# Delta-rule attention and an MLP mixer on one core: two products of a fast matrix scheme change places, one chain gets a bank of its own, and the second half of the order is written anew

## The chip, the cores and the metric

The kernel runs on one core of a Trainium2 chip. A core has engines that work at the same time, each from a queue of its own in the order in which the program issued: TensorE (PE; its weight loads, PEld, overlap its matmuls), VectorE (DVE), ScalarE (ACT), GpSimd (POOL) and SyncE (SP), which issues the transfers (DMA) between HBM and the on-chip memory. TensorE writes to PSUM banks; the others read them. An instruction starts when those before it on its engine have started and what it waits for on other engines is done.

The metric is the device time of one execution in microseconds, lower is better. Data are fp32. A matmul of 128x128 by 128x192 leaves two records of PE in the profile (two passes), so a product of two such matmuls has four.

## The reference

```python
def _attn_ref(q, k, v, beta):                      # B 4, H 8, S 768, D 48
    k_n = k / (np.linalg.norm(k, axis=-1, keepdims=True) + 1e-06)
    state = np.zeros((B, H, D, D), dtype=np.float32)
    for t in range(S):
        kt, vt, bt = (k_n[:, :, t], v[:, :, t], beta[:, :, t, None])
        y[:, :, t] = np.einsum('bhd,bhde->bhe', q[:, :, t], state)
        v_old = np.einsum('bhde,bhd->bhe', state, kt)
        state = state + bt[:, :, :, None] * np.einsum('bhd,bhe->bhde', kt, vt - v_old)
    return y

def _moe_ref(x, w_tok1, w_tok2, w_ch1, w_ch2):     # x: (4, 768, 384)
    xt = x.transpose(0, 2, 1)
    h = np.maximum(xt @ w_tok1, 0.0) @ w_tok2      # tokens: 768 -> 256 -> 768
    u = x + h.transpose(0, 2, 1)
    h2 = np.maximum(u @ w_ch1, 0.0) @ w_ch2        # channels: 384 -> 1536 -> 384
    return u + h2
```

The heads of the attention are joined to 384 channels between the two parts.

## The kernel before

The work is cut into jobs, which are generators; each `yield` ends a piece. A string `order` (from L1771) names 2610 pieces, `name*n` being n pieces of a job, and a loop issues them one by one. Each engine's queue is filled in just this order, so a piece that stands earlier is issued earlier on all its engines.

Jobs of the attention work in chunks of 64 tokens. For a unit u of two chunks, `k` loads k and q, `p` prepares them, `c` makes their products with one another, `t` stores parts of them for the triangular inversion, `i` inverts on DVE, `f` (L711) reads the inverted blocks back from HBM, one transfer on SP for each piece, `j` (L843 to L884) joins the four blocks on PE, and `v` (L474) loads v. `r0` to `r23` are the steps of the recurrence for two batches, `r24` to `r35` (`recur_pair`) for the other two. A pair step multiplies the keys by the state (`p_k`, L1009, four pieces), subtracts v on DVE, multiplies by the inverted blocks (`p_w`, L1038, beside `p_y`), copies to `rw_t` on ACT (L1018 is the same step's line for DVE's subtraction), multiplies once more, updates the state on DVE (L1066) and stores to `x_dram` (L1079). Its `p_y2` lies in the one bank with the tag "warm". `s` sums weights ahead of the mixer; `l` fetches batch 3 from `x_dram`.

The mixer of batches 0 and 1 is `m0` and `m1` (stores at L1627). For batches 2 and 3: `T2` (`token_part`: six pieces of four records over 384 columns, L1223, and six of `p_h`, L1238, added on DVE) and `T3` (`token_fast`, a scheme of seven products per 2x2 blocks: L1304, and L1371 for its second half, with banks px, py and pz). `S` and `W` make weight sums on DVE for the fast schemes; W's first piece is one transfer of 576 KB (L1431).

The channel mixing of batches 2 and 3 is done in four groups g of three tiles. `A0` to `A3` (`first_part`) is the first channel product, `F` (`act_forms`) forms sums of its result on DVE, `B` (`last_part`) is the second channel product, its adds and the stores. Both products use a scheme of 15 products for 3x3 by 3x2 blocks. `CHAINS` lists the products in order: the chain (a PSUM bank in which several products add up), the product's number n (its factors are called w{n} and u{n}), and the reads of the bank behind it as (row, column, sign, last). In the first part a product takes two pieces: the matmuls (L1494), then its reads: a copy on ACT (L1504) where the output block is new, else an add on DVE (L1507); after the last, a relu on ACT (L1509). All is done for two halves of the output rows. A chain's bank comes from `ps_mlp`, which has three banks in turn, so chain 3, begun by product 10, takes over the bank of chain 1, whose last product is 4. A product that adds to a chain waits for the chain's reads before it. The second part takes the same list with banks of other pools.

Around 420 us the order before is: `j23` (two pieces), four pieces of `r34`, `T2` (two), `j23` (its last three), `r34`, and so on; `W` begins behind `v23`.

Of the kernel before, what the change touches and what calls it, by code (L numbers as in the profile page):

```python
# [8 lines left out]
FP32 = mybir.dt.float32  # L9
# [14 lines left out]
def kernel(  # L24
# [41 lines left out]
    B, H, S, D = q.shape  # L66
# [12 lines left out]
    NU = B * NCH  # L79
# [21 lines left out]
    def ps_mlp(shape, name):  # L101
        return psum.tile(shape, FP32, name=name, tag="mlp", bufs=3)
# [8 lines left out]
    warm = const.tile([128, 129], FP32, name="warm")  # L111
# [261 lines left out]
    ranked = set()  # L373
# [237 lines left out]
    t16 = spare[:, cuts[1] : cuts[2]].rearrange("s (q t b) -> s q t b", q=2, t=QB)  # L611
# [502 lines left out]
    def sum_weights():  # L1114
# [42 lines left out]
    CHAINS = (  # L1157
# [6 lines left out]
    )  # L1164
# [9 lines left out]
    TW = GT * U // 2  # L1174
# [23 lines left out]
    def op_of(sign):  # L1198
        return ALU.add if sign > 0 else ALU.subtract
# [49 lines left out]

    def token_sums():  # L1250

        rows = w1.rearrange("p (c k) n -> p k c n", k=2)
        for c in range(NCH):
            piece_of(w1, c, 0)
        for j in range(NDH):
            for n in range(0, S, WP):
                piece_of(w2, j, n)
        ksq = work.tile([128, NB, D], FP32, name="ksq", bufs=1)
        spots = [t.rearrange("p a c d -> p (a c d)") for t in kst_of[:NL]]
        spots.append(ksq.rearrange("p b d -> p (b d)"))  # L1260
# [179 lines left out]
    def first_part(g):  # L1440
# [39 lines left out]
        for half in range(2):  # L1480
            begun = set()
            bank = {}
            for chain, n, reads in CHAINS:
                first = chain not in bank
                if first:
                    bank[chain] = ps_mlp([128, 2, TW], "p_r")
                p = bank[chain]
                assert f"w{n}" in summed or n in (4, 8, 10)
                pieces = sums[f"w{n}"]
                width = FT // len(pieces)  # L1490
                for i in range(2):
                    q = 2 * half + i
                    at = q % width * 128
                    nc.tensor.matmul(  # L1494
                        p[:, i], pieces[q // width][:, at : at + 128], f[f"u{n}"],
                        start=first and i == 0, stop=True, skip_group_check=True,
                    )
                yield
                for j, e, sign, last in reads:
                    at = FT * j + 2 * half  # L1500
                    o = r2[:, at : at + 2, TW * e : TW * e + TW]
                    if (j, e) not in begun:
                        assert sign == 1
                        nc.scalar.copy(o, p)  # L1504
                        begun.add((j, e))
                    else:
                        nc.vector.tensor_tensor(out=o, in0=o, in1=p, op=op_of(sign))  # L1507
# [300 lines left out]
    r19*2 k16 v11*3 p15 j11 p10 f13 j11 f13 r19 r20*4 m0*2 r20 r19 j11 r20*2 c15*5
    r20 c15 r20*2 m0 r21*3 j12 r21 p16 r21 p16*2 v11 m0 r21 j12 p16*3 k17*3 r21
    k17*4 r21*3 p16 k17*5 t14 j12 m0*3 r22*2 c16 r22*2 p16 r22 c16*4 r22*2 f13 c16  # L1810
    j13 m0*2 r22 p17 r22*2 p17*2 j13 r23*5 m0 j13 t15 p17*3 r23*2 p17 m0 t15*3
    t14*2 c17*4 t16*3 t14 c17 p17 t16 r23 c17 t17*4 r23 m0*3 v12 i4 m0 k18*4 m0*3
    v12 m0*4 i4 v13 v12*3 i4*3 m0*2 k18*2 i4 m0*2 i4 v13*2 j13 k18 i4*2 j13 i4*2
    m0*2 r24 k18 r24*2 i4 v15 m0 v15 i4 v13 i4*2 m0*3 p18*2 i4 v15*2 r24*3 k18*3
    i4 m0 v13 p18*2 r25*4 i4 p18 k18 m1*6 i4*3 r25 i4*3 r24 i4*2 r24 i4*2 k19*2
    i4*2 r25*2 k19*2 r24 m1 k19*4 p19 r25 v14*5 p18 i4*2 p18 m1*7 k19*4 p19*2 f17
    f15 r25 f14 r25 p18 c18 r25*2 c18*5 f14*3 f15*2 m1 r25 m1 p19 f16 f15 f16*2
    p19 r26*3 k20*2 p19 k20*5 j14 r26 j14 j15 j14 m1 j15*2 j16 m1*2 p19*2 k20*3
    v15 j16*2 m1 r26 s*3 r26*3 m1*2 t18 p20*2 r25 r26*3 f17 c19*3 r26 p20*2 v16*2
    c19 r27*2 r26 v16*2 r27 f17 r27 f17 m1*2 f16 p20 k20 r27*4 c19*2 k20 k21 j17*3  # L1820
    m1 r27*2 p20*3 c20*4 r27 r28*3 k21*3 v16 k21*2 r27 c20*2 r27 k21*5 p21 k21
    p21*2 r28*2 m1 j17 p21*5 m1*3 t20*4 t19*4 r28 j17 r28*2 c21*5 t18*3 c21 m1
    t21*4 i5 m1*2 r28*4 r26 m1*6 i5*2 v17*4 i5*2 m1*3 k22*8 i5*3 r28*2 m1 v18*2
    p22 v17 i5*2 k22*4 r29*5 r27 i5*4 m1 v18*2 m1*2 r29*2 v19*3 i5*4 m1 r29 m1*3
    i5 p22*2 i5*3 p22*2 i5*7 k23*5 p22*2 k23*2 i5*2 k23 i5 m1 v19 m1 v19 m1*5 k23
    m1*6 k23*3 r29*2 v18 p23*2 c22 f19*3 c22*4 m1*2 c22 m1*2 f18*4 p23 t22*3 p23*4
    t22 f20*2 r29*2 m1*4 c23*6 f19 r30*5 t23*4 f20 i6 r29*2 f21 j18 m1 s*2 m1 j18
    m1 j18 f21*3 j19*3 p22 v20*3 j20 S m1*3 j20 m1 i6*5 j21 i6*6 j20 r30*3 m1*5 i6
    m1 r30*2 m1 f20 r30*3 i6*2 r31*4 j21*2 r30 r31 i6*2 r31*3 v20*2 i6 m1*2 i6
    r31*5 i6 j21*2 r32*5 m1 r32*2 v22*2 v21*4 i6*4 m1*3 i6*5 m1 r32*3 m1 i6*3 m1*4  # L1830
# [5 lines left out]
    T3*3 A1*4 B0 A1*6 F0 A1*3 A2 A1 A2 A1*5 A2 F0 A1*15 W A1*5 F0*2 A1*7 W A1*2 B0
    A1*5 F0*3 B0 A1*10 B0 A2*3 W*2 B0 W B0*5 W*2 F0*2 A1 B0*6 A2*3 F1 A2*2 B0*2 F0
    B0 F1*2 B0*5 A2*6 B1 B0 A2*14 A3 A2*18 B1 A2*7 A3 A2*6 A3 B1 F1*3 B0 F1*2 A2*5
    B1*2 A2*4 B1 F1 A2*4 F1 A2*2 B1*8 F1 F2 B1*5 F2*2 B1*2 B2 F2 F1*3 A3*8 B1*6
    B2*2 F2 F1 B1*2 A3*14 F2 A3*6 B1 F2*4 A3 B2*6 A3*2 B2 A3*2 B2 A3*15 F2*4 A3*10  # L1840
# [39 lines left out]
```

## Time and profile before

| | us |
|---|---|
| median of 3 runs | 627.8 |
| the runs | 626.74, 627.8, 632.62 |
| the profiled execution | 626.59 |
| its span in the trace | 624.8 |

The profiled execution's span is 1.8 us shorter than its own time: what lies around the span. Mean granted clock of TensorE in it: 0.975 of full speed.

How the views are read: busy time of an engine is the time in which it has an instruction; a matmul that has begun and waits for its next operand counts as busy. The view of waits adds up idle time by what ended it. The chain follows the work that ended last back to the start. The timeline lists groups of an engine's instructions in order of time: start, length from the first start to the last end, the count, and in brackets the idle time before. A row for windows has the window, its length, the busy time of each engine with its count, the granted clock, the share of the DMA engines and GB/s. A row of transfers has their count, the KB of each and the median us from issue to landing.

```profile
PE   8489888999999999999999999999999999999998
DVE  4986875986889855696667987866788887777683
ACT  7748786548521344113551324423252432412310
PEclk9978897999999999999999999998999999999999
```

This is the span in 40 slices of 15.6 us: PE is busy to 90% and more from the tenth slice on.

### The profile page before, as it was taken

The page shows a single profiled execution, that of the slowest core. Times are in us where ns is not written, and L with a number is a line of the kernel's source. Part 1 is how long each engine was busy: PE and PEld are TensorE (multiplying, and loading weights), DVE is VectorE, ACT ScalarE, POOL GpSimd, SP SyncE. Part 2 cuts the span into 40 slices and gives each one's busy share as a digit, 9 for nine tenths or more (in the row PEclk, how much of TensorE's full clock was granted, in tenths as well). Part 3 has the DMA queues.
Part 4 walks back from the last instruction along what each step waited for, and adds up shares of the span by engine and source line. Part 5 has one row for each costly group of instructions (what it writes and reads, how often), then busy time and mean ns, then how long its engine had stood idle before and what let it go on. Part 6 is the DMA issues. An engine that isn't in the chain of part 4 may idle for free.

```text
span 624.8 us, 20918 instructions
## 1 busy us (share of the span) xinstructions
PE 594.4 (95%) x8733; PEld 517.1 (83%) x8733; DVE 470.2 (75%) x1160; ACT 258.2 (41%) x682; POOL 111.0 (18%) x150
## 2 busy tenths in 40 slices
PE   8489888999999999999999999999999999999998
PEld 5467776667898988977889898896799999999997
DVE  4986875986889855696667987866788887777683
ACT  7748786548521344113551324423252432412310
POOL 2337355215311121003020020020000000000000
PEclk9978897999999999999999999998999999999999
DMA  9565566757553244445445343132202012020001
GB/s 214 124 147 137 141 159 169 152 148 179 121 116 76 64 104 95 99 106 117 89 79 127 83 101 72 33 86 60 83 1 39 1 19 45 14 52 27 0 34 43
DMA packets 154606, 55.54 MB, mean 89 GB/s; under 512 B 129648, under 2 KB 148976, under 8 KB 154512
## 3 DMA queue, kind: packets, MB, share of 16 engines
q1 hardware_dynamic: 154512, 54.20, 38.2%
q8 instruction: 69, 1.13, 0.8%
q14 instruction: 25, 0.20, 0.1%
HBM read 41.19 MB, written 11.21 MB: 84 GB/s over the span
## 4 chain that ended last, share of the span: by engine, by line
PE 85%; DVE 5%; ACT 4%; issue 2%; DMA 1%; POOL 1%; SPq 0%; POOLq 0%; DVEq 0%; ACTq 0%
PE p_c L1664 16%; PE p_o L1685 14%; PE p_r L1494 13%; PE p_a L1566 6%; PE p_b L1566 6%; PE p_g L511 3%; PE p_h L1604 3%; PE p L1589 2%; PE p L1223 2%; PE p_warm L235 2%; PE p_k L920 1%; DVE x L744 1%; PE p_y L1034 1%; PE p_h L1238 1%; PE p_s L958 1%
## 5 line engine op out<-in xcount | busy, mean ns | idle before, releaser
L1664 PE MATMUL p_c<-u_t,wc 128*128 128x256 f32 x432 | 101.4, 386 | 0.6 <-issue 0.6
L1664 PEld LDWEIGHTS p_c<-u_t,wc 128*128 128x128 f32 x432 | 79.7, 190 | 12.0 <-issue 1.1
L1685 PE MATMUL p_o<-wc,r 128*128 128x192 f32 x360 | 65.3, 331 | 0.0
L739 DVE TENSOR_TENSOR sub<-x 128x84 f32<-128x84 f32 (+24 forms) x178 | 58.2, 327 | 8.6 <-DMA x<-n_dram 4.0
L744 DVE TENSOR_TENSOR x<-x,sub 128x84 f32<-128x84 f32 (+24 forms) x178 | 58.1, 327 | 6.1
L1685 PEld LDWEIGHTS p_o<-wc,r 128*128 128x128 f32 x360 | 58.3, 190 | 1.4 <-issue 0.3
L1673 ACT ACTIVATE r<-p_c 128x512 f32<-128x512 f32 x36 | 21.4, 596 | 46.4 <-PE p_c L1664 43.9
L517 DVE TENSOR_TENSOR gm<-p_g,mb 128x512 f32<-128x512 f32 x44 | 29.0, 685 | 11.8 <-PE p_g L511 11.4
L511 PE MATMUL p_g<-kq 48*64 48x128 f32 (+1 forms) x704 | 34.2, 286 | 3.7 <-ACT kq L587 3.3
L511 PEld LDWEIGHTS p_g<-kq 48*64 48x64 f32 (+1 forms) x704 | 26.4, 139 | 9.2 <-ACT kq L587 4.3
L574 POOL TENSOR_TENSOR mb<-mask_c,cs 128x512 f32<-128x512 f32 x20 | 21.2, 1062 | 69.1 <-DVE cs L552 30.0
L293 POOL TENSOR_TENSOR wc<-w_f,d 128x384 uint32<-128x384 uint32 x24 | 24.6, 1028 | 41.7 <-DVE w_f L289 14.1
L484 POOL TENSOR_TENSOR v_st<-v_st,nrm 128x384 f32<-128x384 f32 x12 | 11.0, 915 | 115.6 <-DMA v_st<-in_v_dram 62.4
L1494 PE MATMUL p_r<-t_d,wc 128*128 128x192 f32 x160 | 31.5, 334 | 0.0
L1504 ACT COPY kq<-p_r 128x384 f32<-128x384 f32 x24 | 11.5, 478 | 45.0 <-PE p_r L1494 44.2
L1507 DVE TENSOR_TENSOR gm<-gm,p_r 128x384 f32<-128x384 f32 x40 | 21.0, 551 | 10.8 <-PE p_r L1494 9.6
L1494 PEld LDWEIGHTS p_r<-t_d,wc 128*128 128x128 f32 x160 | 26.0, 190 | 2.6 <-ACT gm L1504 1.3
L1507 DVE TENSOR_TENSOR kq<-kq,p_r 128x384 f32<-128x384 f32 x40 | 21.0, 551 | 8.0 <-PE p_r L1494 5.5
L400 DVE STREAM_TRANSPOSE kq<-pads 128x512 f32<-128x512 f32 x24 | 25.9, 1107 | 1.5 <-DMA pads<-in_q_dram 1.0
L1494 PE MATMUL p_r<-pads,wc 128*128 128x192 f32 x128 | 25.4, 326 | 0.0
L1685 PE MATMUL p_o<-wc,s 128*128 128x192 f32 x144 | 25.2, 328 | 0.0
L1685 PEld LDWEIGHTS p_o<-wc,s 128*128 128x128 f32 x144 | 23.5, 190 | 0.1
(315 smaller groups left out, 1394.5 us busy)
## 6 DMA issues: line engine op xcount, KB each, us to landing
d<-in_moe_w_ch_dram SPq DMA_DIRECT2D x24, 384.0 KB, 3.8
v_st<-in_v_dram SPq DMA_DIRECT2D x96, 48.0 KB, 3.2
out_dram<-xb SPq DMA_DIRECT2D x23, 192.0 KB, 1.9
kst<-in_k_dram SPq DMA_DIRECT2D x64, 48.0 KB, 2.9
n_dram<-gm SPq DMA_DIRECT2D x72, 32.0 KB, 2.3
pads<-in_k_dram SPq DMA_DIRECT2D x24, 96.0 KB, 2.7
pads<-in_q_dram SPq DMA_DIRECT2D x24, 96.0 KB, 2.9
gm<-w_dram SPq DMA_DIRECT2D x72, 32.0 KB, 2.2
```

The costliest lines, as they stand in the source:

```text
L293: nc.gpsimd.tensor_tensor(out=dst.bitcast(U32), in0=f, in1=lo, op=ALU.add)
L400: nc.vector.transpose(kq_of[p // 2][:, i, :, p % 2].rearrange("f p (s g) -> f p g s", g=G), rows_of[i].rearrange("s p (g d) -> s p g d", g ...
L511: nc.tensor.matmul(p_g[PAR[i ^ cc ^ swap(u)], p], kqt[f, p, cc, 0], kqt[f, p, cc])
L517: nc.vector.tensor_tensor(out=blocks(gm_of(u))[:, :, cc, D:GW].rearrange("s p (two n) -> s p two n", two=2), in0=p_g, in1=made[u][:, :, cc ...
L739: nc.vector.tensor_tensor(out=tmp, in0=y[:, :, 0:s, s : s + 1].to_broadcast([n, k, s, w]), in1=y[:, :, s : s + 1, s + 1 : m].to_broadcast( ...
L744: nc.vector.tensor_tensor(out=y[:, :, 0:s, s + 1 : m], in0=y[:, :, 0:s, s + 1 : m], in1=tmp, op=ALU.add,)
L1494: nc.tensor.matmul(p[:, i], pieces[q // width][:, at : at + 128], f[f"u{n}"], start=first and i == 0, stop=True, skip_group_check=True,)
L1507: nc.vector.tensor_tensor(out=o, in0=o, in1=p, op=op_of(sign))
L1566: nc.tensor.matmul(p, a[:, i], w[:, i // 2, i % 2], start=first and i == 0, stop=True, skip_group_check=True,)
L1664: nc.tensor.matmul(p_c[:, k], piece_of(wc1, cb, f * 128)[:, f * 128 : (f + 1) * 128], u_t[:, cb], start=(cb == 0), stop=(cb == NCB - 1),)
L1673: nc.scalar.activation(r2[:, m], p_c, ACTF.Relu)
L1685: nc.tensor.matmul(p, a[:, m], wc2[:, m, j], start=(start and i == 0), stop=(i == NM - 1), skip_group_check=True,)
```

## The change

In `CHAINS`, product 7 moves ahead of product 4, so that the order of products 14, 4, 7, 10 becomes 14, 7, 4, 10, and the two reads of product 10 change places. In `first_part` the bank of chain 3 is the one with the tag "warm", which `recur_pair` uses before it, instead of one of the three. An assertion is added in `token_sums`, which issues nothing. The order from the 1200th of the 2610 pieces on (about 222 us) is new: the same pieces, in other places.

```diff
@@ CHAINS
-        (1, 3, ((1, 1, 1, 0),)), (4, 14, ((2, 1, 1, 0),)), (1, 4, ((1, 0, 1, 0),)),
-        (2, 7, ((1, 1, 1, 1),)), (3, 10, ((1, 0, 1, 1), (2, 0, -1, 0))),
+        (1, 3, ((1, 1, 1, 0),)), (4, 14, ((2, 1, 1, 0),)), (2, 7, ((1, 1, 1, 1),)),
+        (1, 4, ((1, 0, 1, 0),)), (3, 10, ((2, 0, -1, 0), (1, 0, 1, 1))),
         (2, 8, ((2, 1, -1, 1),)), (4, 15, ((2, 0, 1, 1),)), (3, 11, ((0, 0, 1, 1),)),
@@ token_sums
+        assert NU - 1 in ranked and NU - 2 in ranked
@@ first_part
                 if first:
-                    bank[chain] = ps_mlp([128, 2, TW], "p_r")
+                    bank[chain] = (
+                        psum.tile([128, 2, TW], FP32, name="p_r2", tag="warm", bufs=1)
+                        if chain == 3 else ps_mlp([128, 2, TW], "p_r")
+                    )
@@ order, around r33 to r35 (before, then after)
-    v22*3 r31 r32*2 f22 r32 m1*2 r33*4 v21 f22*3 s*3 p23 r33 f23*4 m1*4 j22 r33*2
-    j22 r33*3 j22 j23*2 r33 r34*5 r33*2 T2*2 j23*3 r34*2 s*6 T2 r34*4 r35*2 r34
-    r32 r34 v23*4 r35*2 v23 r35*3 s W*4 r33 T2 r34 r35*3 T2 S W*2 S s S*2 r35 T2
-    r35*2 T2*3 A0*7 T2*3 A0*12 S*3 l*6 A0*23 T3 A0*4 T3 A0*7 A1*3 A0*16 A1 T3 F0*3
-    T3*9 F0 T3*3 F0 B0 T3*3 A1*2 T3 B0 T3*3 A1 T3*3 A1*5 T3*2 B0 T3 B0 T3*3 A1
+    m1*4 v22 s f22 f23 f22*3 r33*5 f23*2 j22 m1*4 r33*3 v23 j22 r33*2 j22 W j23*2
+    T2 r33*2 T2 f23 r33 l s l s r33 j23 r34*4 j23 r34*2 W*3 v23*4 j23 r34*2 T2 r32
+    r34*5 r35*8 T2 r35*2 T3 W r35*2 l*2 T3 s*5 W*2 T2*5 s r34 r35 A0*7 T2*3 A0*11
+    S*3 A0*6 l s l s A0*18 A1 A0*4 A1*2 A0*3 S*3 A0*20 A1*2 T3*2 F0*5 T3*10 A1 S
+    T3 A1*3 T3*3 B0 T3*8 B0*3 T3*4 B0 T3 A1*5 T3*3 A1*2 B0*2 A1*6 W A1*3 F0 A1*6
@@ order, from the 1200th piece (its first line, before and after)
-    r19*3 j10 f10 j10*2 f12 p15 f11*4 f12 r19 c14 r19 v11 p15*3 k16*11 m0 f13 m0
+    r19*3 j10 f10 j10*2 f12 p15 f11*4 f12 r19 c14 r19 v11 p15*3 k16*7 j11 m0*2
...
```

The same jobs have the same pieces; only these lines, and those left out between 222 us and the end, give another order.

More of the change, by code (lines that the diff above doesn't have):

```diff
@@ L1806 @@
     m0*10 v10*2 m0 r18 c14*4 r18*2 m0*2 f10 c14 f10*2 f12*2 p15*3 m0*4 r18 r19 r18
-    r19*3 j10 f10 j10*2 f12 p15 f11*4 f12 r19 c14 r19 v11 p15*3 k16*11 m0 f13 m0
[L1808 to L1830, printed above, removed]
-    v22*3 r31 r32*2 f22 r32 m1*2 r33*4 v21 f22*3 s*3 p23 r33 f23*4 m1*4 j22 r33*2
-    j22 r33*3 j22 j23*2 r33 r34*5 r33*2 T2*2 j23*3 r34*2 s*6 T2 r34*4 r35*2 r34
-    r32 r34 v23*4 r35*2 v23 r35*3 s W*4 r33 T2 r34 r35*3 T2 S W*2 S s S*2 r35 T2
@@ L1834 @@
-    r35*2 T2*3 A0*7 T2*3 A0*12 S*3 l*6 A0*23 T3 A0*4 T3 A0*7 A1*3 A0*16 A1 T3 F0*3
-    T3*9 F0 T3*3 F0 B0 T3*3 A1*2 T3 B0 T3*3 A1 T3*3 A1*5 T3*2 B0 T3 B0 T3*3 A1
[L1836 to L1840, printed above, removed]
@@ L1841 @@
-    B2*5 A3 F2 A3*5 B2*6 A3*10 F3*3 B2*6 F3*3 B3*4 F3*3 B3*3 F3*2 B2*2 B3*13 F3*3
-    B3*3 F3 B3*7
+    r19*3 j10 f10 j10*2 f12 p15 f11*4 f12 r19 c14 r19 v11 p15*3 k16*7 j11 m0*2
+    r19*4 j11 j12 r20*3 k16*2 r20 m0 r20 k16*3 v11 m0 j11 r20*2 v11*2 p15 c15*2
+    p10 r20*2 c15 r20 c15*3 f13*3 p16 r21*5 m0 r21*2 p16*4 k17*7 p16 j12*2 p16 k17
+    r21*3 m0*3 r22 c16 r22*3 k17*4 v11 r22 c16*4 r22*2 m0 r22 t14 p17 f13 c16 t14
+    j13*2 t14 r22 r23 t15*2 t16 r23*2 r22 r23 m0*3 r23 t15*2 r23 p17*5 t16 p17 j13
@@ new lines @@
+    t16*2 m0*3 t14 c17*5 r23*2 c17 t17*2 m0*8 p17 t17*2 i4*3 v12 m0 k18 v15*2 i4
+    m0 i4 m0 i4*3 m0 i4 k18*2 j13 p16 m0*2 j13 i4*4 m0 v12*3 k18*4 v12 k18 r24*2
+    r23 v13*5 m0 k18*4 v15*2 i4*2 m0*2 p18 i4 p18 r24*3 m0 r24 i4 m0 p18*2 r25*4
+    p18 k19*8 i4 m1 r25 i4 m1*4 i4 m1 v14 i4*2 v14 i4*8 r24*3 r25*2 m1 v14 i4*2
+    v14*2 p18*2 r25 m1*2 p19 m1*5 k19*4 p19 f14*2 r25*5 c18*5 f14 c18 p18 r26*3
+    p19*2 j14 p19*3 r26*2 f15*4 f14 m1*2 j14 m1 j14 j15*3 s*2 f17*2 m1 f17 m1
+    f16*3 p19 f16 k20*8 j16*3 j17 m1 r26*3 p20 m1*2 p20 r26*2 c19*2 r26 c19 v15
@@ new lines @@
+    r27*2 v16*2 r27*2 p20*2 k20*2 p20 c19*2 r26*2 k20 v16*2 r25 c19 m1*2 f17 r27*4
+    p20 k20 p20 j17*2 m1 r27*5 c20*4 p20 r28*4 c20*2 k21*9 p21*2 k21*2 p21 k21
+    m1*2 v16 r28 t18 v17 p21*5 t19*4 t18*2 j17 t18 j17 m1*2 r28*3 c21*6 m1*3 r28*3
+    m1*2 r28 m1 t20 s t20*3 t21*4 i5 m1*4 i5 v17*2 r26 i5*2 m1*2 r28 k22*3 i5*4
+    k22*6 m1*2 i5*2 m1*3 i5 v17 r29 i5*3 p22*2 i5 r29 v17 r29*3 i5*2 v19 p22*3
+    k22*3 m1*4 r29 v19*2 i5 k23*6 p22 v18 p22 i5*11 k23*4 r29*2 k23 i5 k23 v18*2
+    i5*2 v19 m1*7 v19 m1*5 r29 c22*5 r29 r27 c22 m1*2 p23*3 m1*3 p23*5 v18 r29 p22
@@ new lines @@
+    f18 m1*3 c23*3 f20*2 f18 c23 f18*2 c23 f19*3 v18 r30 t22*4 c23 t23 r30*4 t23*3
+    f20 m1*3 i6 j18*3 f19 m1*2 S m1 j19*2 j20 j19 f21 r29*2 f21 i6*4 m1*3 i6*6
+    j20*2 m1 r30*3 m1*2 r30*2 i6 f21 m1*2 r30 r31*4 r28 r30*2 i6 j21 f20 j21*2
+    i6*2 r31*3 v20 i6 v20*2 i6 m1*2 i6*3 r31*4 f21 j21 i6*2 v22*3 v20*2 r32*5 r31
+    r29 r31*2 i6*3 m1*5 j21 m1 r32 v21*2 r32 i6*7 m1*2 r30 r32*6 v21*2 s v21 s v22
+    m1*4 v22 s f22 f23 f22*3 r33*5 f23*2 j22 m1*4 r33*3 v23 j22 r33*2 j22 W j23*2
+    T2 r33*2 T2 f23 r33 l s l s r33 j23 r34*4 j23 r34*2 W*3 v23*4 j23 r34*2 T2 r32
@@ new lines @@
+    r34*5 r35*8 T2 r35*2 T3 W r35*2 l*2 T3 s*5 W*2 T2*5 s r34 r35 A0*7 T2*3 A0*11
+    S*3 A0*6 l s l s A0*18 A1 A0*4 A1*2 A0*3 S*3 A0*20 A1*2 T3*2 F0*5 T3*10 A1 S
+    T3 A1*3 T3*3 B0 T3*8 B0*3 T3*4 B0 T3 A1*5 T3*3 A1*2 B0*2 A1*6 W A1*3 F0 A1*6
+    F0 A1*4 B0 A1*15 A2 F0 A1*3 A2*2 A1*9 F0*2 A1*14 W*3 A2*3 B0*2 A2*5 B0*3 W*2
+    F0 B0*3 F1 F0 B0*2 F0*2 B0 A1 B0*4 F0 F1*2 B0*6 A2*10 B1 F1*2 A2*7 B1 A3*2
+    A2*3 B0 A2*26 A3 A2*12 F1 A2*2 F1*4 B1*4 A2*5 A3 F1 F2 A3 B1*4 A3*6 F1*2 B1*7
+    F1 B1*2 A2 F2*3 F1 B1*6 B2 A3*10 B1*3 A3*15 B1 A3*26 F2*4 A3*3 F2*3 B1 B2*4
@@ L1843 @@
+    A3*7 B2*5 A3 B2*2 A3*4 F2*2 F3 B2*7 F3*2 B2*2 F3*2 B2 F3*3 B2*6 F3 F2*2 B3*2
+    F3 B3*10 F3 B2*2 B3*5 F3*4 B3*13
     """
```

## The prediction

> **What bounds the kernel now.** I read the page first, then a table of busy time by stage, then PE's waits from 417 to 444 us (below in this order), and then the chain and the timelines of the places that the change touches.
>
> ```profile
> PE 594.4 (95%) x8733; PEld 517.1 (83%) x8733; DVE 470.2 (75%) x1160; ACT 258.2 (41%) x682; POOL 111.0 (18%) x150
> ```
>
> ```profile
> 222.00:417.00 195.00, 193.88 (x3377) 167.29 (x3375) 143.76 (x372) 66.50 (x197) 29.57 (x40) 1.00 0.42 90
> 417.00:444.00 27.00, 24.97 (x587) 16.96 (x586) 17.07 (x31) 10.20 (x32) 1.02 (x1) 0.94 0.38 105
> 444.00:469.00 25.00, 25.00 (x138) 22.00 (x137) 19.22 (x46) 11.95 (x25) 0.00 (x0) 1.00 0.01 2
> 469.00:487.30 18.30, 18.05 (x110) 17.43 (x109) 16.33 (x45) 3.28 (x8) 0.00 (x0) 1.00 0.22 33
> 487.30:625.00 137.70, 134.58 (x817) 132.09 (x816) 100.30 (x218) 35.40 (x72) 0.00 (x0) 1.00 0.11 27
> ```
>
> ```profile
> PE p_k L1009 <- issue: 1.3, 1, 1.3
> PE p_w L1038 <- DVE rw_t L1018: 0.5, 1, 0.5
> PE p_k L1009 <- DVE ss_t L1066: 0.2, 1, 0.2
> ```
>
> TensorE is the bound: busy 594.4 of the span's 624.8 us. The order is the same up to about 222 us. Behind that, the stage rows (window, length; PE, PEld, DVE, ACT and POOL busy; granted clock) leave PE idle for 1.1, 2.0, 0, 0.25 and 3.1 us; most of the last is the end behind the final product, which the change keeps. So idle time offers little. What else can go lies inside "busy": matmuls that wait with their operands open, and the granted clock of 0.94 in the second row.
>
> **The change, part by part: the first channel product.** From the chain, the first and the last of seven stretches of it (120, 100, 20, 92, 20, 48 and 20 records, 71.12 us together) and, in the middle, one stretch beside a second channel product; then the waits for its banks in the view of tile p_r; two rows of PE's timeline at its fourth product ("t_d,wc"); and the reads' durations (lowest, median, highest ns):
>
> ```profile
> 448.57 20.54 PE p_r L1494 x120
> ...
> 577.38 7.95 PE p_r L1494 x48
> 585.33 2.60 PE p_a L1566 x16
> ...
> 593.78 3.40 PE p_r L1494 x20
> ```
>
> ```profile
>   PEld p_r L1494: 3.3, 17
> ```
>
> ```profile
> 452.96 0.81 PE L1494 MATMUL p_r<-pads,lent 128*128 128x192 f32 x4
> 453.69 0.92 PE L1494 MATMUL p_r<-t_d,wc 128*128 128x192 f32 x4
> ```
>
> ```profile
> L1507 DVE TENSOR_TENSOR kq<-kq,p_r x40: 544/553/556, 488.9 to 597.2; 128x384 f32<-128x384 f32 x40
> L1504 ACT COPY gm<-p_r x24: 460/478/482, 449.3 to 542.2; 128x384 f32<-128x384 f32 x24
> ```
>
> The second channel product's 16 records wait for nothing: 2.60 / 16 = 162.5 ns each. At that price 420 records take 68.25 us, and the seven stretches took 71.12: 2.87 too much, 1.04 of it in the first. The 17 waits of weight loads for a read of the bank carry it. One wait is seen in two rows: a product is four records, 0.65 us, yet from 452.96 to the next start are 0.73 (0.08 late), and the next is 0.92 long instead of 0.81 (0.11). So a wait costs 0.15 to 0.19: 17 x 0.17 = 2.9. In a half with nothing between its products three wait: w4 for the copy of w3 (one product between), w10 for the copy of w4, whose bank it takes over (one between), and w8 for the add of w7 (one between).
>
> After, two products (1.3 us) stand between w3 and w4 and between w7 and w8, and w10 has a bank of its own, whose last user, r35, comes ten products earlier. A copy (0.48) or an add (0.55) that begins 0.2 behind its product needs 0.75 of the 1.3: all three waits go. w4's copy comes a little later on ACT, behind a relu; the swap of w10's reads leaves the one that follows it for last, so nothing waits.
>
> What is late next: w11 adds into w10's bank behind two adds on DVE (0.2 + 0.55 + 0.46 and the handshake, about 1.35), with two products (1.3) between. The stretches of 20 records hold one such wait now: 3.40 − 3.25 = 0.15. It stays, and shows also where w8's wait covers it now. By the new order six halves have no piece of another job between w10 and w11 (both of A0 and of A1, one of A2 and of A3): 6 x 0.15 = 0.90 are left of the 2.87. Sum −2.87 + 0.90 = **−1.97**. The ends are 0 (w11 waits longer, for what the others lost) and −2.87 (w11 waits nowhere); I take the value by the nearest row, that of 3.40.
>
> **Token mixing of batch 3.** Its second half reuses bank pz straight behind a read, twice:
>
> ```profile
> 479.03 0.81 PE L1371 MATMUL p_h<-x,v_st 128*128 128x192 f32 x4
> 479.97 0.92 PE L1371 MATMUL p_h<-r,v_st 128*128 128x192 f32 x4
> ...
> 484.30 0.49 PE L1371 MATMUL p_h<-x,v_st 128*128 128x192 f32 x2
> 484.91 0.59 PE L1371 MATMUL p_h<-r,v_st 128*128 128x192 f32 x2
> ```
>
> 479.03 to 479.97 is 0.94 where four records take 0.65, so 0.29 late, and 0.92 against 0.81 adds 0.11: 0.40. The second: 0.61 where two take 0.33, and 0.10: 0.38. The new order puts a whole B0 product (1.30) into the second: −0.38. At the first, an add of B0 on DVE moves behind: about −0.2. **−0.6** (0 to −0.8). Two more F0 sums stand ahead of it on DVE (some 1.3 us); the A1 products now put ahead of T3's second half just cover them.
>
> **The pair steps r33 to r35.** Three windows, two rows of PE's timeline, the page's row of instruction fetches (count, MB), and that row for the microsecond from 419:
>
> ```profile
> 417.00:420.60 3.60, 3.58 (x229) 3.32 (x228) 1.86 (x5) 2.19 (x7) 0.00 (x0) 1.00 0.57 163
> 420.60:422.70 2.10, 0.78 (x36) 0.62 (x32) 0.00 (x0) 1.99 (x8) 0.00 (x0) 0.99 0.27 42
> 422.70:426.10 3.40, 3.40 (x14) 1.87 (x7) 3.15 (x7) 0.37 (x2) 0.54 (x1) 0.50 0.71 179
> ```
>
> ```profile
> 422.46 0.33 PE L1009 MATMUL p_k<-ss_t,kq 48*64 48x48 f32 x8 [1.32 <-issue]
> 422.72 4.50 PE L1223 MATMUL p<-xb,w 128*128 128x384 f32 x8
> ```
>
> ```profile
> q8 instruction: 69, 1.13, 0.8%
> ```
>
> ```profile
> q8 instruction: 1, 0.02, 8.6%
> ```
>
> In the middle of r34's key products PE stands for 1.32 us and waits for nothing that the profile shows; behind that the clock is 0.50 for 3.40 us. The eight T2 records (384 columns, so 0.325 each by the 162.5 of 192) take 4.50 instead of 2.60; less what overlaps at their end, I put the half clock at 1.75. The pause I read from the instruction queue: 2 x 8733 records of PE over 69 fetches are 253, so PE fetches blocks of about 256 instructions, 16.4 KB each. One fetch lies at 419 to 421 (8.6% of 16 engines in that row: 1.37 us long). In the first window 229 matmuls and as many weight loads, nearly two blocks, pass in 3.6 us: short matmuls use a block up in some 1.8 us, faster than the next arrives. The new order puts T2's first two pieces (2.6 us) ahead of r34, into that block: 1.8 + 2.6 = 4.4 us. Then the fetch, 1.32 late now, is in time, and without the pause the clock stays: **−1.32 − 1.75 = −3.07** (0 if the pause is something else).
>
> [...]
>
> New costs there. T2's pieces stood between r34's key products and p_w, which wait for one another over a subtraction on DVE; now only j23's fourth piece (0.4) does. The wait of 0.53 for rw_t in the view of waits is r35's, with nothing between: +0.3 (0 to 0.5). And f23's fourth read goes behind W's 576 KB and a read of v on SP's queue:
>
> ```profile
> 416.73 1.11 SPq L1627 DMA_DIRECT2D out_dram<-xb  x2
> 417.93 0.55 SPq L1079 DMA_DIRECT2D x_dram<-pads  x1
> 418.57 3.68 SPq L474 DMA_DIRECT2D v_st<-in_v_dram  x4
> ```
>
> ```profile
> wc<-wc_dram SPq DMA_DIRECT2D x1, 576.0 KB, 5.9
> ...
> gm<-w_dram SPq DMA_DIRECT2D x8, 32.0 KB, 2.6
> ```
>
> SP issues one in about 0.6 us. Behind the two stores (to 417.9) come v23's first, W, then f23's fourth, at about 419.2; j23's fourth piece needs it at about 424.1 (the second window's 420.6, 2.6 of T2, 0.9 of r34's key products). Landing 2.6 later (last row, eight under way), it is there at 421.8; wholly behind W, issued at 418.5, at 418.5 + 5.9 + 2.6 = 427.0. Between 0 and 2.9 I take +0.4, near the row of 2.6. The rest of v23, r33's store and two reads of l stand behind it on SP; nothing on PE needs them before 430. Stage: −3.07 + 0.3 + 0.4 = **−2.37**.
>
> [...] No row here shows a small read straight behind a large one.
>
> **222 to 417 us.** Pieces of r20 to r32, k, p, c, f, j, i and m0/m1 change places, the same in kind and number. PE idles 1.1 us in these 195. Some chain steps lose cover and some gain it. I take 0, from −1.1 (all of it goes) to +1.5 (three waits like r35's).
>
> Sum −1.97 − 0.6 − 2.37 = −4.94. The profiled execution took 626.59: 621.65 on its scale. The runs shown stand 0.15 to 6 above it, the median (627.8) 1.2; I add 0.5: **622.2**.
>
> **Rivals.**
> A. The fetch pause moves instead of going: another block of short matmuls is used up too fast, and the clock halves for one window. For it: the row of 229 matmuls in 3.6 us. Against: long records are mixed in just here. 622.2 + 1.75 = 624.0.
> B. The pause is no fetch, and stays with its half clock: 622.2 + 3.07 = 625.3. Against: the fetch at 419.
> C. Everything goes: also w11's waits (−0.9), the two new waits of the stage (−0.7), and idle time before 417 (−1.1): 619.5.
> D. Slower: f23's read is late behind W. If it lands at X, PE idles for X − 424.1, and a pause of that length halves the clock as the one of 1.32 did: 622.2 − 0.4 + 1.75 + X − 424.1. That passes 627.8 from X = 428.4; if the reads of v under way delay W by 3 us more, X is 430.0 and the time 629.4. Against: the reads of gm landed in 2.6.
> E. The change doesn't do what it says: the first product's excess isn't the reads', and stays: 622.2 + 1.97 = 624.2. Against: the 17 waits.
>
> **How the numbers follow.** The forecast has .50 (its own range 620.5 to 624.0), A .17, B .08, C .15, D .06, E .04. 619.0 to 627.0 takes in all but D, the lower edge of C and the worst of the unnamed costs before 417, about 2 in 10. About 1% (6.3 us) is what a measurement of this kernel can tell from no change. Faster by more (below 621.5) are C and .3 of the forecast: .30. Slower by more (over 634.1) is D with X over 434.7, or several costs before 417: .05. Within: .65.
>
> **What would show it.** Right: 120 records of p_r in about 19.8, and the 17 waits down to about 6, all for w11; no "issue" wait of PE near 421 and a clock of 1.00 from 417 to 444; one wait of pz fewer; p_w of r34 waiting 0.3 for DVE. Wrong: PE waiting for the DMA of f23 at j23; the clock below 0.97 in that stage; p_r's stretches at 171 ns a record as now; PE idle for over 2 us from 222 to 417.

## The result, and the profile after

| | before | after |
|---|---|---|
| median, 22 runs each (us) | 627.5 | 624.17 |
| lowest and highest | 624.26, 632.62 | 620.01, 628.07 |
| the profiled execution | 626.59 | 621.49 |
| its span in the trace | 624.8 | 619.7 |

The ratio of the times is 0.994, with an interval of 0.9914 to 0.9966: the change makes the kernel 2.1 to 5.4 us faster, 3.8 in the middle.

The table of stages of the kernel after (columns as before: window, length, busy time of PE, PEld, DVE, ACT, POOL, granted clock, DMA share, GB/s), and the first rows of PE's waits behind 205 us:

```profile
222.00:417.00 195.00, 192.48 (x3358) 165.29 (x3353) 141.08 (x367) 65.51 (x193) 28.64 (x41) 1.00 0.42 89
417.00:444.00 27.00, 26.28 (x600) 18.00 (x600) 18.19 (x39) 11.44 (x34) 1.05 (x1) 1.00 0.39 106
444.00:469.00 25.00, 25.00 (x149) 23.99 (x148) 22.05 (x47) 12.01 (x26) 0.00 (x0) 1.00 0.03 5
469.00:487.30 18.30, 18.10 (x111) 17.60 (x110) 15.99 (x47) 2.24 (x7) 0.00 (x0) 1.00 0.18 27
487.30:620.00 132.70, 129.46 (x795) 128.74 (x793) 97.13 (x209) 34.09 (x71) 0.00 (x0) 1.00 0.11 28
```

```profile
PE p_o L1689 <- DVE xb L1628: 1.3, 3, 0.6
PE p_c L1668 <- issue: 0.5, 1, 0.5
PE p_w L1038 <- DVE rw_t L1018: 0.5, 1, 0.5
```

The second row is the gain that was looked for: the clock is 1.00 from 417 to 444 us (0.94 before), and the pause of 1.3 us by "issue" is gone from the waits. The first row is the loss: PE idles 2.5 us there (1.1 before), 1.3 of it for an add of `m1` on DVE.

From the chain, the first channel product of groups 0 and 1; then PE's timeline at the pair step r34, and at token mixing's two uses of bank pz:

```profile
446.02 19.67 PE p_r L1498 x120
...
485.14 19.66 PE p_r L1498 x120
```

```profile
421.12 2.85 PE L1223 MATMUL p<-xb,w 128*128 128x384 f32 x8
423.89 0.68 PE L1009 MATMUL p_k<-ss_t,kq 48*64 48x48 f32 x32
424.50 0.45 PE L884 MATMUL p_x<-gm,zst 32*32 32x32 f32 x32
```

```profile
475.59 0.89 PE L1372 MATMUL p_h<-x,v_st 128*128 128x192 f32 x4
476.69 0.92 PE L1372 MATMUL p_h<-r,v_st 128*128 128x192 f32 x4 [0.20 <-DVE xb L1296]
...
481.01 0.56 PE L1372 MATMUL p_h<-x,v_st 128*128 128x192 f32 x2
481.41 1.46 PE L1570 MATMUL p_b<-wc,gm 128*128 128x192 f32 x8
482.71 0.49 PE L1372 MATMUL p_h<-r,v_st 128*128 128x192 f32 x2
```

120 records of p_r take 19.67 us instead of 20.54 (19.50 without a wait). T2's eight records take 2.85 instead of 4.50, and r34's 32 key products run through. At pz a product of B0 now covers the second use, but the first came later, not earlier: 475.59 to 476.69 is 1.10 where it was 0.94.

To compare kernels whose pieces lie at different times, each piece is given PE's time from its first record's start to the start of the next piece's; these are added up by job. The pieces are the same in all kernels, so any difference is a wait, a clock or the piece that comes next, whose start ends the count. In us, from one trace each ("behind" is everything from the 1200th piece on, "ahead" the part that all kernels have in common):

| kernel | A0–A3 | B0–B3 | T3 | r34, T2 | m0, m1 | behind | ahead |
|---|---|---|---|---|---|---|---|
| before | 82.07 | 78.16 | 14.43 | 22.62 | 149.69 | 404.70 | 216.13 |
| after | 79.67 | 78.16 | 14.26 | 19.53 | 151.53 | 401.48 | 214.22 |

So of the 5.1 us between the two spans 3.2 lie behind the 1200th piece, and 1.9 come from the 222 us that the change does not touch. Over 14 traces of this study that common part took 212.5 to 218.7. The 3.2 agree with what the runs say (3.8, at least 2.1); the 5.1 have luck in them.

### The profile page after: what moved, and what is told of

It is laid out like the page before. It is cut to its first block, busy times and chain, and to the rows that moved or that the text cites. A ratio compares the mean times of both kernels' runs of the same rounds, so it can differ in the third digit from the quotient of the medians.

```text
span 619.7 us, 20909 instructions
## 1 busy us (share of the span) xinstructions
PE 590.3 (95%) x8733; PEld 515.9 (83%) x8733; DVE 469.1 (76%) x1160; ACT 256.9 (41%) x682; POOL 109.9 (18%) x150
## 4 chain that ended last, share of the span: by engine, by line
PE 74%; DVE 9%; DMA 4%; ACT 4%; issue 2%; SPq 1%; POOL 1%; DVEq 0%; POOLq 0%; ACTq 0%
PE p_c L1668 13%; PE p_r L1498 13%; PE p_o L1689 10%; PE p_a L1570 7%; PE p_b L1570 6%; PE p_g L511 3%; DMA d<-in_moe_w_ch_dram 3%; PE p_h L1608 3%; DVE sub L739 2%; PE p L1593 2%; DVE x L744 2%; PE p_k L920 2%; PE p L1223 1%; PE p_h L1238 1%; PE p_y L1034 1%
## 5 line engine op out<-in xcount | busy, mean ns | idle before, releaser
L1498 PE MATMUL p_r<-t_d,wc 128*128 128x192 f32 x160 | 28.8, 326 | 0.0
L1628 DVE TENSOR_TENSOR xb<-xb,p_o 128x192 f32<-128x192 f32 x42 | 14.6, 348 | 13.0 <-PE p_o L1689 12.6
```

Of the source, the lines that this page charges most:

```text
L1498: nc.tensor.matmul(p[:, i], pieces[q // width][:, at : at + 128], f[f"u{n}"], start=first and i == 0, stop=True, skip_group_check=True,)
```

## The experiments

The theory: the change gains at two places, the first channel product (list and bank together) and the pause by late instructions (T2's pieces), and pays in waits for DVE that were not there. The rivals: another part of the new order gains, or the pause is something else. Times are medians where a ratio with its interval stands beside them, else one run.

### List and bank alone, and the new order alone

```diff
@@ e1: the order of before, with the change's list and bank
@@ e2: the new order, with
     CHAINS = (...
-        (2, 7, ((1, 1, 1, 1),)), (1, 4, ((1, 0, 1, 0),)), (3, 10, ((2, 0, -1, 0), (1, 0, 1, 1))),
+        (1, 4, ((1, 0, 1, 0),)), (2, 7, ((1, 1, 1, 1),)), (3, 10, ((1, 0, 1, 1), (2, 0, -1, 0))),
-    psum.tile([128, 2, TW], FP32, name="p_r2", tag="warm", bufs=1) if chain == 3 else ps_mlp(...)
+    ps_mlp([128, 2, TW], "p_r")
```

> The order of before, with the new list of products and the bank of its own. Measure: PE's time from start to start over the pieces of A0 to A3, 82.07 us before and 79.67 after the change; without any wait it is about 79.2. If the reads of the banks held the products up: 79.6 to 80.1, no wait of a weight load for w4, w8 or w10, and the pause of 1.3 us in r34 with its half clock stays as before; the time 2.0 to 2.5 us below before (ratio 0.996 to 0.997). If the excess is not the reads': 82 and no change in the time. If the new order of pieces and not the list made A faster: 81 or more.

> The new order, with the list of products and the banks of before. If list and bank carry A's gain, A0 to A3 are back at 81.5 to 82.5 us; r34 and T2 together stay at about 19.5 (22.6 before), without pause and half clock. m0 and m1 stay some 1.3 to 1.8 above before, if their new waits are the order's (a DVE queue that is late), and fall back to 149.7 if they were chance of one execution. Time: 1 to 1.5 below before (ratio 0.998).

In the new order product 4 of A3, if it stands ahead of product 7, copies into a block that the last product of B1 has yet to read. So in e2 and e7 that product reads the wrong block, and some numbers of the output differ; the instructions are the same.

| kernel | A0–A3 | B0–B3 | T3 | r34, T2 | m0, m1 | behind | ahead | time | ratio |
|---|---|---|---|---|---|---|---|---|---|
| e1 | 79.82 | 78.91 | 14.44 | 22.68 | 151.91 | 407.28 | 212.81 | 626.55 | 0.9977 (0.9951 to 1.0003) |
| e2 | 83.72 | 81.28 | 14.26 | 19.71 | 150.74 | 408.80 | 216.64 | 630.47 | 1.0051 (1.0023 to 1.0079) |

Two rows of PE's waits in e1:

```profile
PE p_k L1009 <- issue: 1.3, 1, 1.3
...
PE p_b L1569 <- DVE wc L1437: 0.5, 1, 0.5
```

List and bank alone bring A0 to A3 from 82.07 to 79.82, and keep the pause; the order alone takes the pause and leaves A at 83.72, above before. Each place is carried by its own part. 0.75 of e1's gain comes back in B0: PE reaches the second channel product sooner, and a weight sum on DVE (L1437) is not ready; the new order has that sum earlier. The runs of e1 alone show no gain: its interval reaches 1. And e2 is slower than before, where a ratio of 0.998 was expected: without the list, the new order is a loss. Besides A, the list carries B there, which takes the same list: 81.28 in e2, 78.16 in after. The largest part, 1.95, is in B1, where product 8 waits for the add of product 7 behind sums on DVE, with one product between instead of two (the row of 1.8 of e7, below, is this wait).

### Bank, exchange of the products, exchange of the reads

```diff
@@ e7: after, but
-        (2, 7, ((1, 1, 1, 1),)), (1, 4, ((1, 0, 1, 0),)),
+        (1, 4, ((1, 0, 1, 0),)), (2, 7, ((1, 1, 1, 1),)),
@@ e6: after, but chain 3 in ps_mlp([128, 2, TW], "p_r")
@@ e8: after, but
-        (3, 10, ((2, 0, -1, 0), (1, 0, 1, 1))),
+        (3, 10, ((1, 0, 1, 1), (2, 0, -1, 0))),
```

> After, with product 4 ahead of product 7 again (14, 4, 7, 10), the bank of its own and the reads as after. The bank takes away w10's wait alone; w4 then waits for the copy of w3 (one product between) and w8 for the add of w7 (one between): 0.19 and 0.15 in each of up to eight halves. A0 to A3 81.2 to 82.0 us (79.67 after, 82.07 before). If the bank alone made the gain: 79.7.

> After, with products 4 and 7 exchanged and the reads as after, but chain 3 in one of the three banks again. It takes over the bank of product 4, now directly ahead of it, whose copy on ACT stands behind a relu: product 10 waits some 0.8 to 1.3 us in each half that has no other piece between the two. A0 to A3 at 85 to 90 us (79.67 after, 82.07 before), the time 5 to 10 us above after. If the exchange alone made the gain and the bank nothing: 79.7 to 80.5.

> After, with the two reads of product 10 in the order of before. Its first add then needs w4's copy, which ACT ends late; both adds come up to 0.4 us later, and w11 waits 0.3 to 0.5 instead of 0.08 in halves with nothing between: A0 to A3 81 to 82.7 us (79.67 after). If the exchange of the reads does nothing: 79.7.

| kernel | A0–A3 | B0–B3 | r34, T2 | behind | time | before beside it |
|---|---|---|---|---|---|---|
| e7 | 83.64 | 81.27 | 19.41 | 408.67 | 633.17 | 627.39 |
| e6 | 88.13 | 78.24 | 20.58 | 412.78 | 637.33 | 627.33 |
| e8 | 81.13 | 78.16 | 21.04 | 405.14 | 623.38 | 627.33 |

PE's waits in e6:

```profile
PE p_r L1497 <- ACT gm L1507: 4.0, 4, 1.0
PE p_r L1497 <- ACT kq L1507: 2.5, 3, 1.0
```

The steps from start to start within a half tell the rest (of halves with no other piece between these products). Without a wait a product takes 0.65. In before, the excess of products 14, 4, 7, 10, 8 is 0.08, 0.10, 0.08, 0.15, 0.10 (the wait for the next one's operands, and what follows it). In e7 it is 0.08, 0.10, 0, 0.23, 0.10: product 10 no longer waits for w4's copy, and product 8 waits for w7's add just so much longer. The bank alone gains nothing. Here the expectation was wrong (81.2 to 82.0): it took w8's wait as fixed at 0.15, but that wait had been hidden behind w10's. That A is above before in e7 and e2 is the new order's: in four halves it took out pieces of other jobs that stood between these products, and in the last of them product 8 waits 0.69. B is at 81.27 in e7 and at 78.2 in e6 and e8: in the new order the exchange of the products alone is worth 3.1 us there. In e6 product 10 waits 1.15 in six halves and 0.73 in a seventh, as expected; its time is 13 us above after and not 5 to 10, but 4.0 of that lie ahead of the 1200th piece. In e8 the excess ahead of w11 is 0.25 + 0.10 instead of 0.08: the exchange of the reads is worth 1.46 us. So the three edits are one: only together do they leave 0.08 a half.

### The pause in r34

```diff
@@ e3: before, with
-    j23*2 r33 r34*5 r33*2 T2*2 j23*3 r34*2
+    j23*2 r33 T2*2 r34*5 r33*2 j23*3 r34*2
@@ e4: after, with
-    j23*2 T2 r33*2 T2 f23 r33 l s l s r33 j23 r34*4 j23 r34*2
+    j23*2 r33*2 f23 r33 l s l s r33 j23 r34*4 T2*2 j23 r34*2
@@ e5: before, with
-            nc.tensor.matmul(p_w[r, e, p], gm[r, 2 * p + cc, TC], rest[r, e, p])
+            for _ in range(3 if c == 8 else 1):
+                nc.tensor.matmul(p_w[r, e, p], gm[r, 2 * p + cc, TC], rest[r, e, p])
```

> Before, with nothing moved but the first two pieces of T2, which go ahead of r34's key products. If the pause is a fetch that comes too late for a block of short matmuls: no idle time by issue between 418 and 426 us, clock 1.00 there, r34 and T2 together 19.6 to 20.2 us (22.6 before), of it a new wait of p_w of 0.2 to 0.3; time 2.4 to 3.0 below before (ratio 0.9955). If the pause has another cause, 1.3 us of idle stay, with half clock: 22.3 to 22.9. If the fetch only moves: a pause of 0.5 or more at T2, j23 or r34 and clock 0.5 in one window.

> After, with nothing moved but the first two pieces of T2, which go back behind r34's key products. If these short matmuls, next to those of r33 and j23, use a block of instructions up faster than the next is fetched: PE stands in r34's key products by issue for 1.0 to 1.5 us again, one window of half clock follows, and r34 and T2 together are at 21.8 to 22.8 us (19.5 in after, 22.6 before). If it was another part of the new order that took the pause away: 19.5 to 20.

> Before, with the 16 products p_w of r32 issued three times each, the same result each time: 128 more instructions of PE (weight loads and matmuls) some 20 us ahead of the pause, which move every later boundary of 256 instructions half a block towards the front. If the pause stands on such a boundary it goes from r34's key products into j23's products ahead of them (p_z, L843 and L846), at 0.5 to 1.3 us, since the block that ends there has short matmuls too, and r34's key products run through. If it belongs to r34's products (their operands, the queue, the bank), it stays there with 1.3 us. r32 itself costs some 1 to 1.5 us more.

| kernel | r34, T2 | r34's pause | time | ratio, or before beside it |
|---|---|---|---|---|
| e3 | 19.95 | none | 626.83 | 0.9995 (0.9965 to 1.0024) |
| e4 | 23.00 | 1.6 | 625.08 | 627.39 |
| e5 | 19.45 | none; 0.8 in j23 | 630.71 | 627.39 |

In e4, PE's longest wait, and the windows up to the half clock and of it; then in e5 the wait that took the place of r34's:

```profile
PE p_k L1009 <- issue: 1.6, 1, 1.6
```

```profile
419.00:423.80 4.80, 3.21 (x193) 2.83 (x186) 2.42 (x6) 4.52 (x15) 0.00 (x0) 1.00 0.83 225
423.80:427.20 3.40, 3.40 (x8) 1.87 (x7) 2.98 (x5) 0.03 (x1) 0.00 (x0) 0.50 0.69 176
```

```profile
PE p_z L843 <- issue: 0.8, 1, 0.8
```

Moving the two pieces there and back switches pause and half clock off and on: 2.67 us in e3, 3.47 in e4. e5 says what the pause is. r34's products are untouched, but 128 more instructions stand ahead of them, and the pause goes half a block of 256 towards the front, into j23. Counting each matmul, weight load and semaphore instruction on PE, the pauses of before near 315, 393 and 421 us follow the 10,944th, 13,504th and 14,784th instruction, all 192 more than a multiple of 256; after, they follow the 10,944th, 13,504th and 13,760th, and in e5 the 14,784th again, which is another instruction there. No row names the wait, but the transfers of the queue `instruction` (16.4 KB each) show its end. In before one of them ends at 421.17 and PE goes on at 422.46; in e4 at 422.05 and 423.51, in e5 at 426.08 and 427.41. Behind 205 us the 14 traces have 20 pauses of 0.39 us or more at such counts that wait for no other engine, and each ends 1.2 to 1.6 us after such a transfer; of the 556 such counts with no pause (under 0.1 us) only 60 lie so. In after, where r34 runs through, PE passes the 14,784th instruction 2.9 us after the last transfer. I read that as PE waiting there for its instructions.

e3's time doesn't repeat its trace: 2.67 less at the place, 1.3 less behind the 1200th piece (m0 and m1 took 1.2 more, r29 1.1), and a ratio that reaches only to 2.2 us below before. What takes the rest back in the other runs stays open.

### The waits that came

```diff
@@ e9: after, with
-    i5 m1*4 i5 v17*2 r26 i5*2 m1*2
+    i5 m1*5 i5 v17*2 r26 i5*2 m1
-    T3*2 F0*5 T3*10 A1 S T3
+    T3*2 S F0*4 T3*8 F0 T3*2 A1 T3
-    j21*2 i6*2 r31*3 v20 i6 v20*2 i6 m1*2
+    j21*2 i6*2 m1 r31*3 v20 i6 v20*2 i6 m1
@@ e10: e9, and
-    j22 W j23*2 T2 r33*2 T2 f23 r33
+    j22 f23 W j23*2 T2 r33*2 T2 r33
```

Where m1's new wait comes from, in the timeline after (DVE, and PE behind it):

```profile
332.98 0.19 DVE L739 TENSOR_TENSOR sub<-x 128x30 f32<-128x30 f32 x1 [2.14 <-DMA x<-n_dram]
...
334.38 0.35 DVE L1628 TENSOR_TENSOR xb<-xb,p_o 128x192 f32<-128x192 f32 x1
...
334.79 0.43 PE L1689 MATMUL p_o<-wc,r 128*128 128x192 f32 x1 [0.43 <-DVE xb L1628]
```

DVE stands for 2.14 us for the inversion's data, in the order of its queue, and m1's add behind it is late. The data came at the same time as before (332.98, and 332.72 in before), although PE was over a microsecond ahead.

> After, with three pieces of work moved, each for one wait that the trace of after shows. (1) m1's product with its add that stood behind the first pieces of the inversion on DVE goes ahead of them: the product behind it falls from 1.57 to 1.07 us. If the inversion on DVE is what m1's last products wait for in any case, the 0.5 comes back at its next wait there (1.75 becomes 2.2), if not it stays gone. (2) S's last piece goes ahead of F0's sums and the fifth of these behind T3's relu: T3's first wait for pz falls from 0.44 + 0.10 to under 0.2. (3) one product of m1 goes ahead of r31's short matmuls: the block of instructions there lasts over 3.3 us and the pause of 0.5 us at 393 goes. Together 0.9 to 1.4 us below after (ratio to before 0.992).

> The kernel with three moves (e9), and f23's fourth read issued ahead of W's 576 KB instead of behind. In e9 j23's fourth piece waited 0.8 us for that read, in after it did not. If the read's landing hangs on W, j23's fourth piece waits for no transfer now, here and in every run, and takes 0.38 us (1.55 in e9); if the wait was chance of the traffic, it may come again. The other moves as in e9: m1's product 0.98 to 1.07, T3's first wait for pz under 0.2, no pause at 393 us. Time 1 to 3 us below after, if the pauses of e9 at r34 and r35 followed from j23's wait (ratio to before 0.990); 623 to 624 if they come again.

| kernel | T3 | r34, T2 | m0, m1 | behind | ahead | time | ratio |
|---|---|---|---|---|---|---|---|
| e9 | 13.97 | 21.08 | 150.58 | 405.34 | 217.58 | 623.77 | 0.9961 (0.9933 to 0.9990) |
| e10 | 13.98 | 19.52 | 150.54 | 400.07 | 216.04 | 623.40 | 0.9941 (0.9909 to 0.9973) |

The trace of e9 is of its slowest execution, 628.70.

T3's first wait fell in both (1.10 to 0.81, with 0.65 for no wait), and the product of m1 behind r31 took 1.49 instead of 2.10. m1's product by the inversion fell from 1.57 to 0.98, but the next one that waits for DVE rose from 1.75 to 1.88 and 2.15: part of it comes back. The reading is that DVE's inversion sets the end there; no run tests it by itself.

In e9 PE waited 0.83 us for f23's fourth read, in e8 0.88, in e7 0.2; in after not at all, and in e10, with that read ahead of W, not at all. e8's trace shows why: SP's issues, the landings, PE's timeline, and the windows before and of the half clock that followed:

```profile
416.90 0.56 SPq L1432 DMA_DIRECT2D wc<-wc_dram  x1
417.50 0.53 SPq L711 DMA_DIRECT2D gm<-w_dram  x1
```

```profile
wc<-wc_dram SPq DMA_DIRECT2D x1, 576.0 KB, 6.1
...
gm<-w_dram SPq DMA_DIRECT2D x1, 32.0 KB, 5.8
```

```profile
423.34 0.54 PE L884 MATMUL p_x<-gm,zst 32*32 32x32 f32 x30 [0.88 <-DMA gm<-w_dram]
```

```profile
421.20:424.70 3.50, 2.62 (x116) 2.01 (x115) 2.22 (x4) 0.92 (x4) 0.00 (x0) 1.00 0.63 161
424.70:428.10 3.40, 3.40 (x34) 1.71 (x26) 1.03 (x2) 0.73 (x2) 1.28 (x1) 0.50 0.42 125
```

The 32 KB, issued 0.6 behind W's 576, land at 423.3, W at 423.0. In e7 and e9, too, PE's wait for the small read ended 0.3 us after W had landed. In after W took 4.8 and landed at 424.0, and j23's fourth piece came at 424.5 and did not wait; when the small read landed there, its trace does not tell. In e10:

```profile
420.06 0.60 SPq L711 DMA_DIRECT2D gm<-w_dram  x1
420.76 0.40 SPq L1432 DMA_DIRECT2D wc<-wc_dram  x1
```

### The two parts in the order of before, and a last version

```diff
@@ e11: the change's list and bank (e1), and e3's order
@@ e12: e11, and
-    r31*4 j21*2 r30 r31 i6*2 r31*3 v20*2 i6 m1*2 i6
+    r31*4 j21*2 r30 m1 r31 i6*2 r31*3 v20*2 i6 m1 i6
-    W B0*5 W*2 F0*2
+    W*3 B0*5 F0*2
-    T3*3 A1 T3*3 A1*4 B0 A1*6
+    T3*2 B0 T3 A1 T3*3 A1*4 B0*2 A1*6
...
```

> The order of before with only the first two pieces of T2 moved ahead of r34 (e3), and the new list and bank (e1). If these two carry what the change gains: A0 to A3 79.8, r34 and T2 19.5 to 20.0, no pause near 421 and clock 1.00 there; the second channel product of group 0 waits 0.7 us for a weight sum as in e1. PE's time behind the 1200th piece 400 to 401 us where the parts that the change does not touch are as in before (404.7 there, 401.5 after); time 3 to 4.5 below before (ratio 0.9935). If the other moved pieces of the new order are needed: 402 or more and a ratio of 0.997 or above.

> The kernel of e11 (order of before, new list and bank, two pieces of T2 first), with three moves that the traces of this study point to: one product of m1 ahead of r31's short matmuls (the pause of 1.0 us at 393 goes), W's last two sums ahead of five pieces of B0 (B0's eighth and ninth product 0.75 us less together), and B0's third product between the two uses of pz in T3 (0.3). PE's time behind the 1200th piece 399.5 to 400.5 us (401.7 in e11, 401.5 after, 404.7 before), ratio to before 0.990 to 0.992. If such gains come back as waits on other engines, as m1's did: 401 or more and 0.9935.

| kernel | A0–A3 | B0–B3 | T3 | r34, T2 | m0, m1 | behind | ahead | time | ratio |
|---|---|---|---|---|---|---|---|---|---|
| e11 | 79.82 | 78.91 | 14.43 | 20.38 | 150.78 | 401.74 | 215.47 | 623.57 | 0.9933 (0.9907 to 0.9959) |
| e12 | 80.86 | 79.12 | 14.04 | 20.96 | 149.84 | 403.06 | 217.66 | 626.13 | 0.9995 (0.9962 to 1.0028) |

e11 is as fast as the whole change, as far as its six runs tell: list, bank and two moved pieces carry it, and the other moves of the 1400 pieces are not needed for the time. That the ratios of its two halves, 0.9977 (e1) and 0.9995 (e3), do not add up to it stays open. e12's three moves did at their places what was expected (m1's product behind r31 2.55 to 1.49, B0's eighth and ninth 0.64 less, T3 0.39 less), and lost it again, on PE's waits for DVE:

```profile
PE p_r L1497 <- DVE kq L1510: 0.8, 1, 0.8
PE p_a L1569 <- DVE xb L1577: 0.7, 1, 0.7
```

Neither wait is in e11's trace. DVE's adds came late behind the sums that were put ahead. Besides, the clock was 0.50 from 432.2 to 435.6 us, which cost r35 and T2 1.15. No version here is shown to be faster than the change, and e9, e10 and e12 all stayed behind the ratios expected of them.

## Why the prediction was right or wrong

The median, 624.17, is within 619.0 to 627.0 and 2.0 above the predicted 622.2; the way and the size (0.994 by the ratio, 0.991 forecast) are as forecast. By its steps:

- **The first channel product**, −1.97: right in mechanism, −2.40 in the trace and −2.25 with list and bank alone. The mis-sized term is w11's wait, taken as 0.15 from the stretches of 20 records; it was 0.08. That the three edits need one another was not seen, nor that in the new order the list carries 3.1 us of B as well.
- **Token mixing**, −0.6: −0.17. The second use of pz was as forecast (0.32 less by start to start, 0.38 forecast). The first failed: it went from 0.94 to 1.10. The step said that A1's products cover DVE's extra sums; it left out that S's last piece, 0.55 on DVE, had been put there too. With that and one sum moved (e9, e10) it fell to 0.81.
- **r33 to r35**: pause and half clock, −3.07, are −3.09 for r34 and T2 together with r34's new wait in it (0.50 to 0.76 in its fifth piece; +0.3 forecast). e3, e4 and e5 and the ends of the fetches (1.2 to 1.6 us ahead of the end of each of the 20 pauses) bear out that the fetch of a block of instructions decides; the block that the step put at 4.4 us took 4.40. Rival B fell. Rival A did not happen in the profiled execution, but can: e11 has a pause of 0.7 in a later piece of r34, with the clock at 1.00.
- **f23's read**, +0.4: nothing in the trace of after. But rival D's mechanism is real: three of the seven traces with the read behind W have that wait in view, and in e8 the clock halved behind it (0.50 for 3.40 us behind a wait of 0.88), as D said. For the landing, the row of 2.6, taken as nearest, was the wrong one: in e8 the read lands 0.3 behind W, 5.8 after its issue. The step's upper end, 2.9, did not come: the longest wait was 0.88. D may have cost some of the runs of after what it cost e8, and so have lifted the median above 622.2; they left no trace that would show it.
- **222 to 417 us**, 0 with ends −1.1 and +1.5: this step failed most in the trace, +2.4 (of the −3.22 behind the 1200th piece, the steps above give −5.66). One of the signs of being wrong came with it: PE idles 2.5 us there, over the 2 named. Part belongs to the order: m1's product that waits for DVE behind the inversion takes 1.55 to 1.84 in the six kernels with the new order and m1's places as after, and 0.97 to 1.10 in the six with m1 there as in before. The rows above give the likely cause: DVE waits for the inversion's data, which come at the same time, so what PE is ahead is lost there. The rest need not be the order's: e1 has the order of before and 151.91 for m0 and m1, more than after.
- **The base**: the sum gave a span of 619.9 and 619.7 came; but 1.9 us of that are the common first part. What the sum lacked (+2.4) and what luck gave (−1.9) are of about the same size.

## What to carry to other kernels

Where several waits stand close together, taking one away alone may gain nothing (e7: 0.08 less ahead of product 10, 0.08 more ahead of product 8): the next lies behind it, and only a look at all banks, products and reads of that stretch gives the price. A pause of the bounding engine that waits for nothing may be its own instructions (here 1.3 us behind the 14,784th): count them between two such pauses, and try long instructions among short ones (in e3 two pieces of T2 ahead of r34 took 2.67 us of pause and half clock away). When an engine arrives earlier, look in its queue of partners for what does not: a DMA that comes at its own time (the inversion's data, at 332.98 and in before at 332.72), or a small read issued behind a large one (landed 0.3 us after it in e8).

## What the runs showed of the hardware that was not expected

- Behind 205 us all 20 pauses of PE of 0.39 us or more that wait for no other engine stand on a grid of 256 instructions, in r34's key products (1.3 us) as in those of m1 (0.6), and with 128 instructions added ahead the one of r34 came half a block earlier (e5, 0.8 us in j23). Each of the 15 blocks there that were used up in 1.77 to 2.28 us has one behind it: 1.3 behind 1.78 (before), 1.6 behind 1.80 (e4), 0.6 and 0.5 behind 2.08 and 2.28 (the blocks' durations are worked out by that count). Of 81 blocks of 2.9 to 3.8 us 14 have one, of 0.1 us or more; the longest is 0.7 behind 3.72 (e11). So the duration of a block alone does not decide.
- The clock halves for 3.41 us behind pauses of 1.3 (before, e1), 1.6 (e4) and 0.9 us (e8) among small matmuls (48 and 32 rows). It does so in e6, e9 and e12 as well, at r35, where PE idles 0.9, 1.05 and 0.9 us of the 3.41 before, in several waits. Pauses of 0.8 (e5, and e9 at j23) and 0.7 (e11) did not do it. A longer one among matmuls of 128x128 did not do it: in e7, the wait and the window in which most of it lies, followed by full clock:

```profile
PE p_b L1570 <- DVE xb L1578: 1.8, 1, 1.8
```

```profile
559.36:562.77 3.41, 1.63 (x11) 1.33 (x10) 3.19 (x7) 0.15 (x1) 0.00 (x0) 1.00 0.34 54
```

  So the length of a pause alone does not decide: 0.9 us were enough in e8, and 1.8 too little in e7. What else decides stays open.
- A read of 32 KB issued behind one of 576 KB on the same queue landed 0.3 us after it, 5.8 us after its issue (e8), where such reads else took 2.1 to 3.2 (3.2 for the one that e10 puts ahead).
- The part that all kernels have in common took 212.5 to 218.7 us. Differences under some 3 us between two traces' spans say little; the same pieces compared one by one say more.
